# Transposing the late queries of four heads ahead of the expert matmuls, in an attention-and-experts kernel

## Chip, cores, metric

One core of one Trainium2 chip. The metric is the device time of one execution in microseconds (us), the median of several. "PE" is TensorE, "DVE" VectorE, "ACT" ScalarE, "POOL" GpSimd. L252 is line 252 of the kernel; the lines named here are the same ones in both kernels.

## The reference

```python
# q, k, v: (4, 8, 768, 64); centroids: (8, 16, 64)
q_assign = argmax(einsum('bhsd,hcd->bhsc', q_n, c_n))      # rows normalized; likewise k_assign
mask = q_assign[:, :, :, None] == k_assign[:, :, None, :]
attn = softmax(where(mask, scale * q @ k.T, -1e9))          # per batch and head
x = (attn @ v).transpose(0, 2, 1, 3).reshape(3072, 512)
p = domain_probs / (domain_probs.sum(-1, keepdims=True) + 1e-9)
out = sum(p[:, e:e+1] * (relu(x @ w1[e]) @ w2[e]) for e in range(4))
```

Each query and key picks one of 16 clusters; attention runs inside a cluster; four dense experts of 512 to 1024 to 512 follow.

## The kernel before

The order of instructions is fixed by hand. Attention is a generator of "steps" (scores on PE, an exponential on ACT, the product with v on PE two steps later). The first 22 steps run alone; then expert matmuls are woven between further steps. Work on later queries is hung on step numbers (`at_step`) or on a paced generator.

A **turn** takes raw fp32 queries through four 128 x 128 transposes on PE into one PSUM bank and a copy of the bank:

```python
        def turn(self, y, copy, shared=False):          # class Assign, cut
            tp = self.bank()                            # next of self.tags
            for x in range(m):
                for i in range(self.i0, self.i1):
                    nc.tensor.matmul(tp[:, c0:c0 + 128], raw[...][:, y * m + x, i * 128:(i + 1) * 128],
                                     ident, is_transpose=True)              # L242
            t32 = moe.tile([128, DM], F32, name="t32q", tag="oacc", bufs=4)
            copy(t32, tp[:, :m * w])                                        # L252
            ...
        # cast: copies 64 rows of t32 to bf16, on GpSimd                    # L260
```

Each pair of heads is normalized on DVE and turned by PE for the experts:

```python
                        def finish():                                       # cut
                            nc.vector.reciprocal(zr, av[:, :, :, D:D + 1])              # L683
                            nc.vector.tensor_tensor(xn, av[...], zr..., op=ALU.mult)    # L685
                            def turn():                                     # a step or two later
                                nc.tensor.matmul(tp[...], xn[...], identb, is_transpose=True)  # L692
                                dve(xTs[u][...], tp[...])                               # L697
```

The expert weights psb come from four small DVE operations (`probs`: L856, L857, L859, L861). Where things hang:

```python
    at_step = {
        ...
        19: lambda: (qc.onehot(), qc.keep(), qc.send_all()),
        21: probs,
        86: lay_late_constants,
    }
    def late_queries():                  # paced over steps 22 to 32, among the experts
        load_raw()
        for y in (0, 1):
            qd.turn(y, dve, True)
            yield
        casts(qd, (0, 1))
        load_raw(3)
        qd.scores(dve)
        yield
        ...
```

The softmax here doesn't subtract the row's maximum and nothing guards it: scores larger than these inputs give would overflow.

Of the kernel before, what the change touches and what calls it, by code (L numbers as in the profile page):

```python
# [20 lines left out]
def kernel(  # L21
# [22 lines left out]
    QT = A // 2  # L44
# [29 lines left out]
    act, dve, pool = nc.scalar.copy, nc.vector.tensor_copy, nc.gpsimd.tensor_copy  # L74
# [35 lines left out]
    def late(t, b):  # L110
        x = KF[b % 2].rearrange("p h r c -> p (h r c)")
        n = NP * A * 128
        return x[:, t * n:(t + 1) * n].rearrange("p (x i r c) -> p x i r c", i=QT, r=2, c=128)
# [15 lines left out]
    def load_part(b, t, g, js=slice(0, HG), c=slice(0, A * D)):  # L129
        nc.sync.dma_start(  # L130
            out=raw[b, t, g][:, js, c],
            in_=(q, k, v)[t][b, g * HG:(g + 1) * HG]
            .rearrange("h (p a) d -> p h (a d)", p=128)[:, js, c])

    def take_raw():
        nonlocal loaded
        x = ORDER[loaded]
        loaded += 1
        raw[x] = raws.tile([128, HG, A * D], F32, name="raw")
        return x  # L140

    def load_raw(n=1, upto=len(ORDER)):
        for _ in range(n):
            if loaded < upto:
                load_part(*take_raw())
# [198 lines left out]
    class Crossed(Assign):  # L344
# [41 lines left out]
        def casts(self):  # L386
            y = self.g * HG // 2
            if self.b < ROWS:
                for r in range(2):
                    self.cast_half(r)  # L390
                return
            dve(late(self.t, self.b)[:, y:y + HG // 2], self.rows_of())
# [413 lines left out]

    k0, k1 = Assign(0, 1, 0, ("s", "mo", "mo", "mo")), Assign(0, 1, 1, ("s", "misc"))
    qa, qb = Assign(0, 0, 0, ("av",), 0, 1), Assign(0, 0, 1, ("mo",), 0, 1)
    qc, qd = Assign(0, 0, 0, ("misc", "mo"), 1, QT), Assign(0, 0, 1, ("misc",), 1, QT)
    for j in range(HG):  # L810
        k0.turn(j, act)
    lay_centroids()
# [40 lines left out]
    def probs():  # L853
        nonlocal psb
        dps = consts.tile([128, B * A], F32, name="dps")
        nc.vector.tensor_reduce(dps, dp.rearrange("p b a e -> p (b a) e"), axis=AX.X, op=ALU.add)  # L856
        nc.vector.tensor_scalar_add(dps, dps, 1e-9)  # L857
        dpr = consts.tile([128, B * A], F32, name="dpr")
        nc.vector.reciprocal(dpr, dps)  # L859
        psb = consts.tile([128, B * A, E], F32, name="psb")  # L860
        nc.vector.tensor_mul(psb, dp.rearrange("p b a e -> p (b a) e"),  # L861
                             dpr[:, :, None].broadcast_to([128, B * A, E]))

    psb = None
    def late_casts():
# [16 lines left out]
        14: lambda: (casts(qc, (0, 1)), qc.scores(dve)),  # L882
        16: lambda: (qc.back(), qc.top()),
        19: lambda: (qc.onehot(), qc.keep(), qc.send_all()),
        21: probs,
        86: lay_late_constants,
    }

    def late_queries():
        load_raw()  # L890
        for y in (0, 1):
            qd.turn(y, dve, True)
            yield
        casts(qd, (0, 1))
        load_raw(3)
        qd.scores(dve)
        yield
        qd.back()
        qd.top()
        yield  # L900
        qd.onehot()
        qd.keep()
        qd.send_all()
        yield
    S1 = PER_U + PAUSE
    gens.append(Paced(late_queries(), 5, S1 - 6, S1 + 4))
    for b in range(1, B):
        gens.append(Paced(assigns(b), XSTEPS[b], PER_B * (b - 1) if b > 1 else S1 + 7,
# [55 lines left out]
```

## Time and profile before

| | before |
|---|---|
| median of the first three runs | 472.22 us (472.22 to 472.25) |
| span in the profile | 470.4 us |
| PE busy | 463.2 us, 98% |
| chain that ended last, on PE | 95% |

The span is PE's time; every other engine has slack in the mean (ACT is busy 59% of the span, DVE 48%, POOL 41%). So the change is read from PE's idle moments. The prediction shows the lines. Two of its terms come back below: the **stretch** from the attention transposes at 26.7 us (L692) to the first expert matmul of the second unit (L739, at 35 us), in which everything that the change moves lies, and the four small operations in it:

```profile
28.76 0.24 DVE L856 TENSOR_REDUCE dps<-dp 128x24 f32<-128x96 f32 x1
29.03 0.18 DVE L857 TENSOR_SCALAR dps<-dps 128x24 f32<-128x24 f32 x1
29.25 0.30 DVE L859 RECIPROCAL dpr<-dps 128x24 f32<-128x24 f32 x1
29.58 0.26 DVE L861 TENSOR_TENSOR psb<-dp,dpr 128x96 f32<-128x96 f32 x1
```

(start, duration, engine, line). From the first to the L683 behind them, at 29.76, it is 1.00 us.

### The profile page before, as it was taken

Reading aid. Unit: us, or ns where it says so; the run is one execution under the profiler, and the core shown is the slowest. Engines: PE = TensorE matmul, PEld = TensorE weight load, DVE = VectorE, ACT = ScalarE, POOL = GpSimd, SP = SyncE. Lnnn points to the kernel's source line nnn. Section 1 sums busy time; section 2 is a strip of 40 time slices with the busy share of each in tenths; the row PEclk is TensorE's granted clock in tenths of the full one; section 3 lists DMA queues with packets and bytes.
Section 4 is the critical chain, followed back from the end, with each engine's and each line's share of the span. In section 5 each row is a group of like instructions: output and inputs, shape, how many; then the busy total and the mean of one; then the engine's idle time right before and its main releaser. Section 6 shows DMA issues by size and latency. Waiting matters only on the chain.

```text
span 470.4 us, 11349 instructions
## 1 busy us (share of the span) xinstructions
PE 463.2 (98%) x4505; PEld 329.1 (70%) x4505; DVE 227.4 (48%) x554; ACT 276.9 (59%) x502; POOL 194.8 (41%) x301
## 2 busy tenths in 40 slices
PE   8999999999999999999999999999999999999996
PEld 5778777767767766777776667766766666667665
DVE  5964723542325563321234463523778767674112
ACT  5767675445655655566565656656665675664342
POOL 5936779275355593450433942000233232230000
PEclk9999999999999999999999999999999999999999
DMA  8999966996645941503666844220100100100101
GB/s 277 262 211 339 216 99 120 236 127 182 144 68 127 182 114 32 144 18 61 169 123 127 133 106 151 71 75 11 52 13 8 54 11 10 33 29 11 46 2 45
DMA packets 82381, 49.85 MB, mean 106 GB/s; under 512 B 57944, under 2 KB 77080, under 8 KB 82328
## 3 DMA queue, kind: packets, MB, share of 16 engines
q1 hardware_dynamic: 73080, 39.80, 35.1%
q0 software_dynamic: 8576, 9.25, 11.0%
q8 instruction: 35, 0.57, 0.5%
q14 instruction: 18, 0.15, 0.1%
q10 hardware_dynamic: 672, 0.08, 0.1%
HBM read 37.31 MB, written 6.30 MB: 93 GB/s over the span
## 4 chain that ended last, share of the span: by engine, by line
PE 95%; DVE 2%; DMA 1%; issue 0%; ACT 0%; SPq 0%; ACTq 0%
PE ps_mo L739 36%; PE ps_mo L758 35%; PE ps_s L649 9%; PE ps_av L676 7%; PE ps_s L562 1%; DMA kf<-oht 1%; PE ps_misc L562 1%; PE ps_s L87 1%; PE ps_mo L406 1%; PE ps_mo L242 1%; PE ps_misc L406 1%; DVE kf L315 1%; PE ps_misc L242 1%; PE ps_mo L267 0%; PE ps_misc L267 0%; DVE oh L287 0%
## 5 line engine op out<-in xcount | busy, mean ns | idle before, releaser
L655 ACT ACTIVATE at<-ps_s 128x512 bf16<-128x512 f32 x252 | 147.6, 596 | 115.5 <-PE ps_s L649 100.1
L739 PE MATMUL ps_mo<-xT,w1b 128*128 128x256 bf16 (+1 forms) x1664 | 195.9, 264 | 0.0
L758 PE MATMUL ps_mo<-w2b,hT 128*128 128x512 bf16 (+2 forms) x784 | 190.0, 375 | 0.0
L739 PEld LDWEIGHTS <-w1b 128*128 128x128 bf16 x1664 | 146.1, 98 | 24.8 <-issue 1.2
L745 ACT ACTIVATE hT<-ps_mo 128x512 bf16<-128x512 f32 x192 | 114.7, 598 | 60.5 <-PE ps_mo L739 57.7
L767 DVE SCALAR_TENSOR_TENSOR oacc<-ps_mo,psb,oacc 128x512 f32<-128x512 f32 (+1 forms) x74 | 54.3, 734 | 125.3 <-PE ps_mo L758 125.1
L758 PEld LDWEIGHTS <-hT 128*128 128x128 bf16 x784 | 66.9, 98 | 57.8 <-issue 3.1
L649 PE MATMUL ps_s<-qf,kf 80*128 80x256 bf16 (+1 forms) x456 | 82.7, 267 | 0.8 <-ACT at L655 0.4
L676 PEld LDWEIGHTS <-at 128*128 128x128 bf16 x1152 | 69.9, 97 | 15.3 <-issue 1.7
L676 PE MATMUL ps_av<-vx,at 128*128 128x65 bf16 x1152 | 80.3, 193 | 0.0
L662 POOL TENSOR_TENSOR at<-at,same 128x512 bf16<-128x512 bf16 x24 | 28.2, 1177 | 98.5 <-ACT at L655 83.0
L649 PEld LDWEIGHTS <-kf 80*128 80x128 bf16 x456 | 42.1, 98 | 20.6 <-issue 1.4
L380 POOL COPY t<-t 128x768 uint16<-128x768 uint16 x40 | 44.3, 1127 | 0.0
L579 DVE TENSOR_SCALAR same<-qf,late 128x256 bf16<-128x256 bf16 x144 | 39.0, 323 | 0.0
L662 DVE TENSOR_TENSOR at<-at,same 128x512 bf16<-128x512 bf16 x48 | 21.6, 450 | 25.9 <-ACT at L655 25.9
L364 POOL COPY h<-raw 128x768 uint16<-128x768 uint16 x24 | 20.3, 864 | 30.4 <-DMA raw<-in_k_dram 16.7
L361 POOL COPY h<-raw 128x768 uint16<-128x768 uint16 x16 | 13.1, 829 | 39.3 <-DMA raw<-in_q_dram 32.3
L765 DVE TENSOR_SCALAR oacc<-ps_mo,psb 128x512 f32<-128x512 f32 x18 | 13.5, 748 | 27.0 <-PE ps_mo L758 27.0
L683 DVE RECIPROCAL zr<-ps_av 128x4 f32<-128x4 f32 (+1 forms) x50 | 8.9, 178 | 33.3 <-PE ps_av L676 33.2
L336 POOL DMA_DIRECT2D qf<-oht x40 | 20.4, 519 | 7.5 <-DVE oht L313 3.9
L422 POOL COPY st<-sct 128x384 uint16<-128x384 uint16 x16 | 11.0, 736 | 28.8 <-DMA sct<-scs 28.8
L685 DVE TENSOR_TENSOR xn<-ps_av,zr 128x256 bf16<-128x256 f32 (+1 forms) x50 | 20.7, 414 | 1.7
(130 smaller groups left out, 263.2 us busy)
## 6 DMA issues: line engine op xcount, KB each, us to landing
raw<-in_v_dram SPq DMA_DIRECT2D x8, 768.0 KB, 5.4
out_dram<-oacc SPq DMA_DIRECT2D x23, 256.0 KB, 2.0
raw<-in_k_dram SPq DMA_DIRECT2D x7, 768.0 KB, 7.5
raw<-in_q_dram SPq DMA_DIRECT2D x6, 768.0 KB, 5.7
w1b<-in_moe_w_dram POOLq DMA_DIRECT2D x4, 1024.0 KB, 12.3
w2b<-in_moe_w_dram POOLq DMA_DIRECT2D x4, 1024.0 KB, 17.6
qf<-nos SPq DMA_DIRECT2D x2, 768.0 KB, 5.2
xT<-xn SPq DMA_TRANSPOSE x80, 2.4
```

The lines of the kernel that those rows point to most:

```text
L336: (nc.gpsimd if self.b or self.i0 and self.g else nc.sync).dma_start(out=self.rows(slice(D, D + CL), j, r), in_=self.oht[p0:p0 + CL, :self.w])
L380: pool(self.all[:, y * w:(y + 1) * w].bitcast(U16)[:, z::2], self.t16[:, (2 * z + y) * w:(2 * z + y + 1) * w])
L579: nc.vector.tensor_scalar(same[:, x * 256:(x + 1) * 256], clusters(b)[:, g, w, k // 2, k % 2, :], key_nos[b % 2][:, g, 8 * i + 4 * (k // 2 ...
L649: nc.tensor.matmul(sp[:, x * n:(x + 1) * n], KF[b % 2][:K, h, r, i * 128:(i + 1) * 128], QF[b % 2][:K, h, rs[0]:rs[-1] + 1, w * 128:(w + 1 ...
L655: nc.scalar.activation(at, sp, ACT.Exp, scale=scale)
L662: (nc.gpsimd if n4 in POOL_STEPS else nc.vector).tensor_tensor(at, at, same_cluster(b, w, cur), op=ALU.mult)
L676: nc.tensor.matmul(av[:, h % 2, m, :], at[:, c0:c0 + 128], VX[b % 2][:, h, 2 * i + r, :], start=(first and x == 0 and m == 0), stop=(last ...
L685: nc.vector.tensor_tensor(xn[:, :nr].rearrange("p i j d -> p j i d"), av[:, :, :, :D], zr.broadcast_to([128, 2, nr, D]), op=ALU.mult)
L739: nc.tensor.matmul(ph[:, x * n:(x + 1) * n], W1[e][:, i, (f + x) * 128:(f + x + 1) * 128], xT[:, i, :], start=(i == 0), stop=(i == ND - 1))
L745: nc.scalar.activation(ht, ph, ACT.Relu)
L758: nc.tensor.matmul(po, hT[f // per][:, c0:c0 + 128], W2[e][:, f, c], start=(f == 0), stop=(f == NF - 1))
L767: nc.vector.scalar_tensor_tensor(oacc[:, c], po, pap, oacc[:, c], op0=ALU.mult, op1=ALU.add)
```

## The change

Both turns of the late queries of heads 4 to 7 (`qd`) go ahead of the experts, where PE has idle moments; their casts follow at once. The intent is to take 8 transposes out of the stretch in which PE never waits.

```diff
-    qc, qd = Assign(0, 0, 0, ("misc", "mo"), 1, QT), Assign(0, 0, 1, ("misc",), 1, QT)
+    qc, qd = Assign(0, 0, 0, ("misc", "mo"), 1, QT), Assign(0, 0, 1, ("misc", "mo"), 1, QT)
...
-        21: probs,
+        18: lambda: qd.turn(0, dve, True),
+        21: lambda: (qd.turn(1, dve, True), casts(qd, (0, 1)), probs()),
...
     def late_queries():
         load_raw()
-        for y in (0, 1):
-            qd.turn(y, dve, True)
-            yield
-        casts(qd, (0, 1))
+        yield
         load_raw(3)
+        yield
         qd.scores(dve)
```

## The prediction

> **What bounds the kernel now.** I read the page's busy times and chain first, then the waits of TensorE (PE) in two stretches, then the timeline of the place that the diff touches.
>
> ```profile
> PE 463.2 (98%) x4505; PEld 329.1 (70%) x4505; DVE 227.4 (48%) x554; ACT 276.9 (59%) x502; POOL 194.8 (41%) x301
> ...
> PE 95%; DVE 2%; DMA 1%; issue 0%; ACT 0%; SPq 0%; ACTq 0%
> ```
>
> PE is the bound, by busy share and by the chain that ended last. So the question is which idle moments of PE the change fills or makes. The waits of PE from 17 to 60 us are these; from 60 us to the end the same view has no line at all.
>
> ```profile
> PE ps_misc L296 <- DVE oh L287: 0.6, 2, 0.4
> PE ps_s L649 <- ACT at L655: 0.4, 2, 0.3
> PE ps_mo L692 <- DVE xn L685: 0.3, 1, 0.3
> PE ps_s L649 <- DMA kf<-oht: 0.3, 1, 0.3
> ```
>
> After about 38 us PE never waits. A delay there goes to the end undiminished, and so does a gain. PE's idle time ahead of the experts (which start at 28.77) is small: about 0.3 us in each of few places. The place itself, from the timeline (start, duration, engine, line):
>
> ```profile
> 26.72 0.23 PE L692 MATMUL ps_mo<-identb,xn 128*128 128x128 bf16 x1 [0.28 <-DVE xn L685]
> 26.79 0.39 PE L649 MATMUL ps_s<-qf,kf 80*128 80x128 bf16 x4
> 27.45 0.29 DVE L313 TENSOR_SCALAR oht<-ps_mo 128x256 bf16<-128x256 bf16 x1 [0.24 <-PE ps_mo L296]
> 27.80 0.17 DVE L683 RECIPROCAL zr<-ps_av 128x2 f32<-128x2 f32 x1
> 27.92 0.39 PE L649 MATMUL ps_s<-qf,kf 80*128 80x128 bf16 x4 [0.16 <-ACT at L655]
> 28.00 0.29 DVE L685 TENSOR_TENSOR xn<-ps_av,zr 128x128 bf16<-128x128 f32 x1
> 28.35 0.23 PE L692 MATMUL ps_mo<-identb,xn 128*128 128x128 bf16 x1
> 28.77 0.61 PE L739 MATMUL ps_mo<-xT,w1b 128*128 128x128 bf16 x8
> 29.56 0.63 PE L242 MATMUL ps_misc<-ident,raw 128*128 128x128 f32 x4
> 29.76 0.17 DVE L683 RECIPROCAL zr<-ps_av 128x2 f32<-128x2 f32 x1
> 29.97 0.29 DVE L685 TENSOR_TENSOR xn<-ps_av,zr 128x128 bf16<-128x128 f32 x1
> 30.03 0.61 PE L739 MATMUL ps_mo<-xT,w1b 128*128 128x128 bf16 x8
> 30.23 0.69 DVE L252 COPY t32q<-ps_misc 128x512 f32<-128x512 f32 x1
> 30.83 0.22 PE L692 MATMUL ps_mo<-identb,xn 128*128 128x128 bf16 x1
> 31.45 0.63 PE L242 MATMUL ps_misc<-ident,raw 128*128 128x128 f32 x4
> 31.92 0.61 PE L739 MATMUL ps_mo<-xT,w1b 128*128 128x128 bf16 x8
> ```
>
> A "turn" is four fp32 transposes on PE (L242) and a copy of the bank on VectorE (L252). The reader is to see its two turns at 29.56 and 31.45, between expert matmuls, and the other VectorE work: each attention output goes L683, L685 on VectorE, L692 on PE, so L692 can make PE wait for VectorE (it did at 26.72).
>
> [...] four transposes show 0.63 us, but the next matmul starts 0.47 us after the first (29.56 to 30.03), so a turn costs PE 0.47 us, and 8 bf16 matmuls of 128 columns 0.45 us. [...] the scores behind the waiting L692 started only after it. So a copy put ahead of L683 on VectorE delays L692, and transposes put behind a waiting L692 don't fill its wait. [...]
>
> **The change, part by part.** Nothing is added or removed: the order of instructions shows equal counts on every engine, and differences on PE and VectorE only (GpSimd, ScalarE and the DMA queues keep theirs). What moves: turn 0 goes behind the L692 of 26.72, ahead of the scores of 26.79; turn 1 behind the L692 of 28.35, ahead of the scores of 28.41. On VectorE, copy 0 comes ahead of the L313 of 27.45; copy 1 comes ahead of the four small operations (28.76 to 29.76, the expert weights psb) and thus ahead of the L683 of 29.76. The banks of this head group alternate between "mo" and "misc"; I read from the built program what each first write of a bank waits for, and each is a reader done long before.
>
> PE moves 2 x 0.47 = 0.94 us of work from the saturated stretch to the stretch before. The gain is what of it falls into idle time; I replay the stretch with the trace's durations. Turn 0 runs 26.80 to 27.27. It stands behind the wait at 26.72, so does not fill it. The scores move from 26.79 to 27.27, their exponential from 27.27 to 27.75, and the scores that wait for that exponential from 27.92 to 28.40: this gap of 0.33 (27.59 to 27.92 before, counted by streaming time) moves along and isn't filled. Both shift by 0.47 to 0.48. VectorE: copy 0 starts at 26.80 + 0.63 + 0.04 = 27.47; start to start such copies took 0.59 to 0.70 in this trace, so L313 is at 28.06 to 28.17, L683 at about 28.4, L685 at 28.6 to 28.9, and L692 at about 28.95 (0.06 after L685's end). PE would be ready at 28.74 (28.40 + 0.22 + 0.12). That is a wait of 0.2 against 0.09 before: **+0.1**.
>
> Turn 1 runs from 29.02 to 29.49, the experts start at about 29.84, 1.07 later than before. Copy 1 starts at 29.02 + 0.67 = 29.69; the four small operations at 30.3 to 30.4; they take 1.00; L683 at 31.3 to 31.4; L685 ends 0.50 later, at 31.8 to 31.9; L692 at about 31.9. In PE's order that L692 comes 30.83 + 1.07 - 0.47 (the turn no longer at 29.56) = 31.43. So PE, until then without a gap, waits some **+0.45**. Then turn 1's old place (31.45) falls away, -0.47. The next L692 (33.35) finds its L685 done: no VectorE copy stands at 32.19 any more. The score matmuls (L267), now in bank "mo", wait for an ACT result of 33.8 and come at 34.1. Nothing else changes; the gap before the one-hot transposes at 37.20 stays.
>
> Sum: +0.94 (turns early) - 0.94 (turns gone later) + 0.1 + 0.45 + 0 filled = +0.55 us. [...] I add a little for start-to-start times on the longer side: +0.6, so 472.22 + 0.6 = **472.8 us**.
>
> **Rivals.** First, the intent: the turns fall into idle time of PE ahead of the experts. For it: there are gaps of 0.28 and 0.33 close by, and ScalarE, which the scores feed, has slack. At most 0.94 is gained, 471.3 us. Against: the turns stand behind one wait, and push the matmuls that start the other. Second, VectorE becomes the bound for longer: copy 0 also delays the one-hot result (L313), whose eight transfers feed the scores at 35.40, and the late raw loads behind these on the same queue. For: the transfers start 0.6 late, and if these scores waited for them, another 0.5 to 1 us would be lost, 473.5 us. Against: the page has 4.8 us to landing, the first two are due at about 34, and those scores need only them. Third, a wash: VectorE overlaps better than I replay (the small operations or L683 start sooner), the new wait vanishes: 472.2 to 472.3 us. I hold the replay at about 65%, the wash 15%, the gain 10%, the larger loss 10%.
>
> **Range and chances.** No rival reaches 2% (9.4 us): the work moved is 0.94 us, and the largest loss named is 1.3. So "within 2%" is 0.99. The range goes from the wash, 472.1, to a replay with each wait 0.3 longer, 473.4.
>
> **What would show it.** In the profile after: PE's wait at L692 for VectorE's L685 appears once more, some 0.4 us at about 31.9 (step two); the wait at 26.72 is still there, with L242 right behind it; the gap before the scores at 28.4 is still there (nothing filled); experts start at 29.8 instead of 28.77; PE's position at the second half of the first expert is some 0.55 later than before and stays so to the end. Wrong it would be if the L692 of 31.9 shows no wait, if the gaps at 26.7 to 28.4 vanish from PE's waits, or if PE gets new waits after 38 us, which the replay says it does not.

## The result, and the profile after

After: 473.48 us median of 4 runs (472.98 to 473.64); before, beside it: 472.24 (472.22 to 472.28). The ratio is 1.0024, with a 95% interval of 1.0007 to 1.0042. Ratios here are the mean time of one kernel's runs over that of the other's of the same rounds, so not quite the ratio of the medians. It is within 2%, and slower.

PE's waits from 17 to 60 us in the changed kernel (engine, line, whom it waited for: us in total, times, longest):

```profile
PE ps_mo L692 <- DVE xn L685: 0.8, 1, 0.8
PE ps_s L649 <- DMA kf<-oht: 0.6, 2, 0.4
PE ps_s L649 <- ACT at L655: 0.4, 2, 0.3
PE ps_misc L296 <- DVE oh L287: 0.4, 1, 0.4
PE ps_mo L296 <- DVE oh L287: 0.2, 1, 0.2
```

Before, the one wait at an L692 was the 0.3 us of 26.72. Now it is 0.8 us, at a later L692: the one of 32.61 in the timeline of the changed kernel (lines picked from the view):

```profile
27.16 0.23 PE L692 MATMUL ps_mo<-identb,xn 128*128 128x128 bf16 x1
27.23 0.61 PE L242 MATMUL ps_mo<-ident,raw 128*128 128x128 f32 x4
28.81 0.38 PE L649 MATMUL ps_s<-qf,kf 80*128 80x128 bf16 x4 [0.16 <-ACT at L655]
29.24 0.23 PE L692 MATMUL ps_mo<-identb,xn 128*128 128x128 bf16 x1
29.30 0.61 PE L242 MATMUL ps_misc<-ident,raw 128*128 128x128 f32 x4
30.02 0.69 DVE L252 COPY t32q<-ps_misc 128x512 f32<-128x512 f32 x1 [0.29 <-PE ps_misc L242]
30.10 0.61 PE L739 MATMUL ps_mo<-xT,w1b 128*128 128x128 bf16 x8
30.63 0.24 DVE L856 TENSOR_REDUCE dps<-dp 128x24 f32<-128x96 f32 x1
30.77 1.26 POOL L260 CAST qf<-t32q 64x512 bf16<-64x512 f32 x2 [0.88 <-DVE t32q L252]
30.90 0.51 DVE L857 TENSOR_SCALAR dps<-dps 128x24 f32<-128x24 f32 x1
31.45 0.30 DVE L859 RECIPROCAL dpr<-dps 128x24 f32<-128x24 f32 x1
31.79 0.36 DVE L861 TENSOR_TENSOR psb<-dp,dpr 128x96 f32<-128x96 f32 x1
32.07 0.16 DVE L683 RECIPROCAL zr<-ps_av 128x2 f32<-128x2 f32 x1
32.26 0.29 DVE L685 TENSOR_TENSOR xn<-ps_av,zr 128x128 bf16<-128x128 f32 x1
32.61 0.23 PE L692 MATMUL ps_mo<-identb,xn 128*128 128x128 bf16 x1 [0.76 <-DVE xn L685]
```

The reader is to see three things. The two turns stand right behind an L692, and the gap before the scores of 28.81 is still there. The small operations now come behind the copy of 30.02, and two of them are longer: L857 took 0.51 us (before 0.18) and L861 0.36 (before 0.26), while two casts ran on GpSimd (0.61 us each, the first to about 31.4, where L857 ended too). From L856 to L683 it is 1.44 us instead of 1.00. And L692 waits for the L685 at the end of this row. (The first L692, of 27.16, did not wait in this profile, since a transfer had just held PE for 0.21 us; in the repeat below it waits 0.34 us again.)

Where the time went, by the stretch: its end is this line, before and after,

```profile
34.95 0.61 PE L739 MATMUL ps_mo<-xT,w1b 128*128 128x128 bf16 x8
36.27 0.61 PE L739 MATMUL ps_mo<-xT,w1b 128*128 128x128 bf16 x8
```

so 26.72 to 34.95 is 8.23 us before, 27.16 to 36.27 is 9.11 after, **+0.88 us**. The other part of the 1.24 us between the medians lies ahead of it: the stretch starts 0.44 us later, and of this 0.4 was lost in the first 8 us, ahead of anything that the change touches. The first nine transposes of the kernel (of keys), before and in the changed kernel:

```profile
4.63 1.74 PE L242 MATMUL ps_mo<-ident,raw 128*128 128x128 f32 x9
4.58 2.12 PE L242 MATMUL ps_mo<-ident,raw 128*128 128x128 f32 x9
```

The experiments had to tell whether this belongs to the change.

### The profile page after: what moved, and what is told of

Same layout as the page of the kernel before. It is cut to its first block, busy times and chain, and to the rows that moved or that the text cites. A ratio compares the mean times of both kernels' runs of the same rounds, so it can differ in the third digit from the quotient of the medians. Undisturbed runs are those within 1.5% of the kernel's fastest.

```text
span 471.7 us, 11348 instructions
## 1 busy us (share of the span) xinstructions
PE 463.2 (98%) x4505; PEld 329.7 (70%) x4505; DVE 227.1 (48%) x554; ACT 277.0 (59%) x502; POOL 194.3 (41%) x301
## 4 chain that ended last, share of the span: by engine, by line
PE 95%; DVE 3%; DMA 1%; issue 0%; ACT 0%; SPq 0%; DVEq 0%; ACTq 0%
PE ps_mo L739 35%; PE ps_mo L758 35%; PE ps_s L649 9%; PE ps_av L676 7%; PE ps_s L562 1%; DMA kf<-oht 1%; PE ps_mo L242 1%; PE ps_misc L562 1%; PE ps_s L87 1%; PE ps_mo L406 1%; PE ps_mo L267 1%; PE ps_misc L406 1%; DVE kf L315 1%; DVE oh L287 0%; DVE mx L284 0%; PE ps_misc L242 0%
## 5 line engine op out<-in xcount | busy, mean ns | idle before, releaser
L683 DVE RECIPROCAL zr<-ps_av 128x4 f32<-128x4 f32 (+1 forms) x50 | 8.9, 178 | 34.9 <-PE ps_av L676 34.9
L685 DVE TENSOR_TENSOR xn<-ps_av,zr 128x256 bf16<-128x256 f32 (+1 forms) x50 | 20.7, 414 | 1.7
```

Source lines behind the costliest of these rows:

```text
L685: nc.vector.tensor_tensor(xn[:, :nr].rearrange("p i j d -> p j i d"), av[:, :, :, :D], zr.broadcast_to([128, 2, nr, D]), op=ALU.mult)
```

## The experiments

All gave correct results. Each was timed in five rounds against the kernel before on its chip. The times turned out to have an uneven start (below), so the stretch in the trace, which does not hold it, is the better measure of a few tenths. For the last versions, whose first turn lies ahead of the stretch, a longer one is used, from the score transposes at about 25 us (L276) to the same end. Each stretch is read from one profiled execution. Two pairs show how well it repeats: 8.23 in before and in hold24, which has the same stretch, and 9.11 and 9.10 in the changed kernel and its repeat. The longer one also holds waits for a transfer, which differ: probs_late, with the short stretch of before, has 10.25 there against 10.02.

A diff below that shows `- 21: probs` or `hold_clock` is against the kernel before, any other against the changed kernel.

| kernel | times, us (lowest, median, highest) | stretch, us | longer stretch, us |
|---|---|---|---|
| before (29 runs beside these, on three chips; a median for each) | 472.03; 472.49, 472.18, 472.19; 473.03, and one of 474.42 | 8.23 | 10.02 |
| after_again | 472.98, 473.06, 473.65 | 9.10 | 10.90 |
| probs_late | 472.06, 472.17, 472.96 | 8.22 | |
| casts_act | 472.60, 472.84, 473.30 | 8.67 | |
| before_probs_late | 472.30, 472.72, 473.24 | 8.44 | |
| turn0_early | 472.18, 472.46, 472.71 | 8.20 | |
| turn1_early | 472.91, 473.06, 473.56 | 9.07 | |
| turns_ahead | 471.92, 471.99, 472.10 | | 9.60 |
| turns_ahead_again | 471.73, 471.92, 472.27 | | 9.58 |
| ahead_probs_kept | 471.82, 471.94, 472.35 | | 9.90 |
| turns_ahead_split | 471.50, 471.82, 471.86 | | 9.18 |
| hold24 | 472.85, 473.26, 473.60 | 8.23 | 10.03 |

The run of 474.42 shows a mean granted clock of 0.995, the other runs of before 0.999 or 1.000; it is in the ratios of turns_ahead, ahead_probs_kept, turn0_early and turn1_early. Without it, the plain ratios of the means would be 0.9994, 0.9995, 1.0004 and 1.0018.

**after_again: the changed kernel once more.**

> The changed kernel once more, for its spread. In its profile the first nine transposes ran 0.4 us slower than in the kernel before, ahead of anything that the change touches. Theory A (the change itself costs 0.9 us, at the attention transposes of 32.6 us; the slow start is separate and differs from run to run): times between 473.0 and 473.7, and a profile whose delay against before grows by 0.9 us between 26 and 34 us, whatever its start. Rival B (the slow start is most of the loss): runs with a fast start come within 0.3 us of before, at about 472.5.

Ratio 1.0016 (1.0002 to 1.0030). Four of five runs came at 472.98 to 473.09; of the nine runs of before beside them, four came at 472.10 to 472.19 and the rest up to 473.03. So the low groups are 0.9 us apart, and both kernels have slower runs: the slow start is no part of the change. Its profiled run, 473.03, had a fast start:

```profile
4.58 1.63 PE L242 MATMUL ps_mo<-ident,raw 128*128 128x128 f32 x9
```

and a stretch of 9.10 us. Theory A holds (0.87 us in the stretch, whatever the start); rival B falls.

**probs_late: the small operations behind the third normalization.**

```diff
-        21: lambda: (qd.turn(1, dve, True), casts(qd, (0, 1)), probs()),
+        21: lambda: (qd.turn(1, dve, True), casts(qd, (0, 1))),
+        23: probs,
```

> The changed kernel, with the four small VectorE operations (expert weights psb) moved behind the normalization of the third output, so that copy 1 no longer pushes them ahead of it. Theory A: the wait of TensorE of 0.76 us at the attention transposes near 32.6 us vanishes, the kernel is 0.9 us faster than the changed one run beside it, and within 0.2 us of before (apart from the start). Rival C (the early transposes themselves cost TensorE time that is not won back): the time stays at that of the changed kernel, 0.9 us or more above before.

Ratio 0.9997 (0.9985 to 1.0010). The stretch is 8.22 us, that of before. The profiled run (472.96) is the slowest of the five, with a slow start (2.14 us for the nine transposes) and a longer wait for a transfer ahead of the stretch; the other four came at 472.06 to 472.19. The attention transposes no longer wait:

```profile
31.99 0.22 PE L692 MATMUL ps_mo<-identb,xn 128*128 128x128 bf16 x1
```

So the whole loss is that one wait. And with it gone the change is a wash: 0.9 us of transposes moved ahead of the experts win nothing, since they fill no idle moment there.

**casts_act: the casts on ScalarE, later.**

```diff
-        21: lambda: (qd.turn(1, dve, True), casts(qd, (0, 1)), probs()),
+        21: lambda: (qd.turn(1, dve, True), probs()),
...
+        for y in (0, 1):
+            for r in range(2):
+                qd.cast(y, r, act)
         qd.scores(dve)
```

> The changed kernel, with the four casts of the late queries on ScalarE, later, instead of on GpSimd at 28.6 to 32.0 us. In the changed kernel two of the small operations took 0.51 and 0.36 us (0.18 and 0.26 before) while a GpSimd cast ran. Theory A1 (the casts block them): they are back at 0.18 and 0.26 us, the wait near 32.6 us shrinks from 0.76 to about 0.35 us, and the time falls by 0.4 us against the changed kernel. Rival (their length is of another cause, such as their distance to the copy): they stay at 0.5 and 0.36 us and the time stays.

The stretch is 8.67 us: 0.44 less than in the changed kernel, 0.44 more than before. In its timeline both operations are short again, and the wait is 0.32:

```profile
30.77 0.18 DVE L857 TENSOR_SCALAR dps<-dps 128x24 f32<-128x24 f32 x1
...
31.32 0.26 DVE L861 TENSOR_TENSOR psb<-dp,dpr 128x96 f32<-128x96 f32 x1
...
32.04 0.23 PE L692 MATMUL ps_mo<-identb,xn 128*128 128x128 bf16 x1 [0.32 <-DVE xn L685]
```

Ratio 1.0009 (0.9997 to 1.0022): by the times alone, this isn't told from before, nor clearly from the changed kernel; by the trace it is half-way. So half of the loss (0.44 us) is the order on DVE, and half goes with GpSimd's casts at the same time. How a cast lengthens an operation on DVE, no trace shows; the traces show which operations took longer. In the changed kernel L857, a tensor_scalar on 24 numbers per partition, took 0.51 us and ended 0.03 us behind the first cast. L856, a reduction, kept its 0.24 us in the run probs_late, where it ran at 31.81 us under the second of two casts that began at 31.07. L859, a reciprocal, kept its 0.30 us beside a cast in the changed kernel (31.45) and in ahead_probs_kept (30.24).

casts_act takes the casts to another engine and to a later time at once, so by itself it shows only that they did it. The other traces close the gap. In six profiles whose timelines show L857 beside a cast (after, after_again, probs_late, before_probs_late, turn1_early, ahead_probs_kept), it took anything from 0.29 to 0.51 us, and ended 0.03 to 0.04 us behind the end of that cast each time; in four whose timelines show none beside it (before, casts_act, turns_ahead, turn0_early) it took 0.18. L861 beside a cast took 0.35 or 0.36 us and ended 0.11 to 0.12 behind it (five profiles), and 0.26 in the five others of these ten. A length of another cause, the rival, would not follow the cast's end.

**before_probs_late: the control.**

```diff
-        21: probs,
+        23: probs,
```

> Control: the kernel before, with the small VectorE operations moved to the same later place. There the attention transposes at 30.8 us did not wait. Theory A: no change, within 0.1 us of before. If it gains as much as the same move gains in the changed kernel, then the move is good by itself and says nothing of the change.

The expectation of "no change" missed: the stretch is 8.44, 0.21 more than before. In the trace the moved operations now fall under the casts of turn 0 (L857 0.51, L861 0.36 us), and the copy of turn 1 and the fourth normalization come later behind them. But the control says what it was made for: the move is no gain by itself. The ratio, 1.0005 (0.9993 to 1.0018), tells nothing.

**turn0_early and turn1_early: one turn each.** In turn0_early one turn is hung on step 18, in turn1_early one on step 21; the second one stays in the generator, with its casts for both. (turn0_early has the two alternating banks of the changed kernel, turn1_early the one bank of before.)

```diff
+        18: lambda: qd.turn(0, dve, True),                  # turn0_early
-        21: probs,                                          # turn1_early
+        21: lambda: (qd.turn(0, dve, True), probs()),       # turn1_early
...
-        for y in (0, 1):                                    # both
-            qd.turn(y, dve, True)
-            yield
+        yield
+        qd.turn(1, dve, True)
+        yield
```

> Turn 0 alone at its new place (ahead of the experts), turn 1 where the kernel before has it. Theory A: turn 0 fills no gap and copy 0 is off the path of the later normalization, so its 0.45 us are only moved: within 0.1 us of before, no new wait near 31 us. Rival (either early turn costs half of the loss): 0.45 us slower.

> One turn alone at the place of turn 1 (the second of the two is left where the kernel before has it). Theory A: this copy stands ahead of the small operations and its casts block two of them, so the whole loss is here: a wait of about 0.8 us at the attention transposes near 31 us, 0.85 us slower than before. Rival: 0.45 us slower.

The stretch is 8.20 us with turn 0 early (before 8.23) and 9.07 with the one at the place of turn 1 (after 9.11); ratios 1.0001 (0.9987 to 1.0015) and 1.0015 (1.0000 to 1.0031). The whole loss is the place of turn 1, ahead of the small operations; its L857 took 0.51 us there too. Turn 0 is only moved.

**turns_ahead: a step earlier.** If an early turn gains only what falls into a gap, it must come ahead of the wait, not behind it.

```diff
-        18: lambda: qd.turn(0, dve, True),
+        17: lambda: qd.turn(0, dve, True),
-        21: lambda: (qd.turn(1, dve, True), casts(qd, (0, 1)), probs()),
+        20: lambda: (qd.turn(1, dve, True), casts(qd, (0, 1))),
+        23: probs,
```

> A version that should beat both: turn 0 one step earlier, ahead of the scores that precede the attention transposes of 26.7 us, so that TensorE does it while VectorE normalizes; turn 1 one step earlier, ahead of the scores that wait for an exponential (the gap of 0.33 us at 27.6); the small operations behind the third normalization. Theory A (early turns gain only what falls into a gap of TensorE): turn 0 is free, turn 1 costs about 0.12 of its 0.45 us, so 0.6 us faster than before between runs of equal start, some 471.5 us, and 1.5 us faster than the changed kernel. Rival (the scores delayed by turn 0 delay their exponential and all after it): within 0.2 us of before.

The longer stretch is 9.60 us, 0.42 less than before; the expected 0.6 was too much. The waits at the attention transposes are gone, and one of the two for an exponential. The missing 0.2 is in the first expert group, 0.83 us instead of 0.61:

```profile
29.24 0.83 PE L739 MATMUL ps_mo<-xT,w1b 128*128 128x128 bf16 x8
```

Its fourth matmul reads the second output, whose copy (L697, 29.36 to 29.57) now stood on DVE behind the copy of turn 1 (from 28.76). By time, the ratio is 0.9991 (0.9977 to 1.0005): not told from before. In order, though, its six runs (471.92 to 472.10) lie below ten of before's eleven (472.11 and more; one is 472.03).

**ahead_probs_kept: the same, with `21: probs` left.**

> The same, but with the small VectorE operations left where the change leaves them, ahead of the third normalization. Theory A: copy 1 now comes earlier, so these end at about 30.4 us even when a GpSimd cast blocks two of them, and the attention transposes near 30.5 us wait some 0.4 us: 471.9 us. If the place of the turns is all that matters, the time is that of the run before this one.

The longer stretch is 9.90: 0.30 more than without, where 0.4 was expected. L857 took 0.38 us, L861 0.36, and L692 came 0.30 us behind what precedes it on PE (31.40, where the products before it were through at 31.10). The times of the two (471.94 and 471.99 in the median) don't tell them apart; the start is uneven by more.

**turns_ahead_split and turns_ahead_again.** In the first, PE's part of turn 1 stays on step 20, and its copy and casts go to step 21 (the diff is against turns_ahead):

```diff
-        20: lambda: (qd.turn(1, dve, True), casts(qd, (0, 1))),
+        20: lambda: qd.turn(1, lambda *x: held.append(x), True),
+        21: lambda: (dve(*held.pop()), casts(qd, (0, 1))),
```

> The version with both turns one step earlier, with one more repair: in its trace the first expert group took 0.83 us instead of 0.61, since copy 1 stood on VectorE ahead of the copy of the second output that this group reads. Here TensorE's part of turn 1 stays and its copy goes behind that one. Theory A: the group is back at 0.61 us, and from the score transposes at 25 us to the second unit's first expert matmul it takes 9.4 us (before 10.02, both turns ahead 9.60): 0.6 us faster than before at equal starts. Rival (copy 1, later, delays the third normalization again): a wait at the attention transposes near 31 us, and no gain over 9.60.

> The version with both turns one step earlier once more: its trace says 0.42 us faster than before, its times only 0.2, with a start of middling speed in its profile (nine first transposes 2.01 us; 1.63 in fast starts, 2.14 in slow ones). If the start is what hides the rest, runs with a fast start come at 471.7 us, and the profile shows 9.6 us for the stretch again.

The split version beats both kernels: 471.82 us median, ratio 0.9985 (0.9972 to 0.9999), longer stretch 9.18 us, its first expert group at 0.61 us again. It is 0.2 shorter than expected: the four scores behind turn 0 took 0.39 us here, and 0.65 in turns_ahead, where the last of them started late (0.56 in its repeat). The program has these scores wait for one-hot keys sent by DMA, and in four other profiles such a wait is named there (`DMA kf<-oht`, 0.21 to 0.74 us), so a sooner landing is likely, though not shown, and need not repeat. It also gives some back at 40.85 us, in a wait that no other kernel here had, for the next batch's keys:

```profile
40.85 0.55 PE L242 MATMUL ps_misc<-ident,raw 128*128 128x128 f32 x3 [0.26 <-DMA raw<-in_k_dram]
```

The repeat of turns_ahead had its stretch at 9.58 again, and two runs at 471.73 and 471.74, 0.4 below the low group of before (472.13 to 472.19). Its profiled run, 472.27, had the slowest start of all (2.15 us). The ratio is 0.9989 (0.9977 to 1.0002). So the uneven start can hide a gain of this size in the medians.

**hold24: the uneven start.** The kernel begins with 16 matmuls on zeros; here 24, in the kernel before.

```diff
-    hold_clock(16)
+    hold_clock(24)
```

> The kernel before with 24 instead of 16 matmuls on zeros ahead of the first transposes, to see what the uneven start is. If it is the rate at which TensorE runs in its first microseconds (the first transposes came at 0.21 us each in slow starts and sped up at another moment in each run), the first nine transposes, which start some 1.7 us later, take at most 1.6 us in any run, and the times of the runs lie within 0.3 us of each other, about 1.5 us above before. If the uneven start comes from the loads, the spread stays.

The ratio is 1.0016 (1.0003 to 1.0029). The nine transposes took 1.27 us in the profile, but the times spread over 0.75 us (472.85 to 473.60), as much as before's, where 0.3 was expected, and the median lies 1.07 us above before's, where 1.5 was. By the expectation's own words a spread that stays speaks for the loads. Yet it does not settle it: in the profile all 24 matmuls came about 0.21 us apart, 5.3 us in all, as the 16 do, and PE sped up only with the transposes behind them; if it does so at another moment in each run, the 24 end at another moment too. What stands is a correlation. Of the ten other experiments, the three profiled runs whose nine transposes took 1.60 to 1.70 us lie within 0.06 us of their kernels' fastest run; those with 1.81 to 2.15 lie 0.1 to 0.9 above. The traces show the delay itself: over all twelve profiles with 16 matmuls, the score transposes near 25 us (L276) start at 24.79 to 24.98 us where the nine took 1.60 to 1.81, and at 25.14 to 25.45 where they took 2.01 to 2.15. What sets PE's rate at the start, no run shows: the transposes came about 0.21 us apart at first in a slow start (after: 5.65 to 6.50 us, four of them) and 0.11 to 0.12 later, among other matmuls, while the granted clock read 1.00 from the start in the six profiles that were read by stages (before, after and the first four experiments), whose nine transposes took 1.63 to 2.14 us.

## Why the prediction was right, and where it was off

The mechanism was right, and so was the direction. One term of its sum was too small by half. That a copy ahead of L683 on DVE delays L692 was the expectation; in the changed kernel the copy, the four small operations, L683 and L685 started one after the other from 30.02, and L692 came at 32.61.

- **"Turns fill no gap"**: right. After, both turns stand behind an L692, the gap before the scores of 28.81 is there, and probs_late (8.22 against 8.23 us) shows that moving the turns alone is a wash.
- **"A turn costs PE 0.47 us"**: 0.44 and 0.45 at the new places (27.23 to 27.67, 29.30 to 29.75), so 0.05 less for both together.
- **"+0.1" at the second L692**: nothing. The scores, from 28.81, and the products behind them take PE to 29.15, and L692 comes at 29.24: 0.09, as before. The next operation on DVE started 0.60 us after the copy did, and L683 0.20 behind that; the prediction left 0.59 to 0.70 open for the first and took some 0.3 for the second.
- **"+0.45" at the third L692**: this is the mis-sized term. Without a wait it would follow the products of 31.57 at 31.69; it came at 32.61, so it lost **0.92 us** (the profile counts 0.76, from the end of its record of these products, at 31.85). The prediction's step "the four small operations take 1.00" failed: they took 1.44. It moved the casts on GpSimd with the turns, and said that GpSimd's order doesn't change, but not that its casts would run at the same time as these operations, nor that two of them would take longer there (0.51 us instead of 0.18, 0.36 instead of 0.26). casts_act takes just that away and gets 0.44 back; what it leaves at the third L692, 0.44 in the stretch and 0.05 for the shorter turns, is about the 0.45 of the replay.
- **The sum**: 0.92 for the wait, less 0.05 for the shorter turns, is 0.87; the stretch has 0.88. Predicted was +0.6.
- **The range**: 472.1 to 473.4 left out the spread that goes with the uneven start, up to about 0.9 us between runs of one kernel. The first runs of before were all alike within 0.06 us and gave no hint of it. So the median of 473.48 consists of the 0.88 us and about 0.4 us of start. That it is just the figure of the rival of the transfers (473.5) is a coincidence: its mechanism did not come (below).
- **Rivals**: the gain (turns in idle time) did not come at these places, but did when the turns were put ahead of the waits. The transfers (one-hot rows later) did not matter: the scores that need them, at 36.72 us, did not wait. No new wait of PE appeared after 38 us; the one at L296, 38.52, is that of 37.20 before.

## What to carry to other kernels

Here work moved to a busy engine's idle time helped only where it stood *ahead* of the wait in that engine's order (turns_ahead: 0.42 us less in the longer stretch); behind it, it just moved the wait along (probs_late: 8.22 us in the stretch, 8.23 before). Look also at the engine that takes the result: here a copy ahead of a normalization on VectorE, with the casts that followed it, cost PE 0.92 us, as much as the eight transposes take. And when a producer moves, its followers on other engines move with it: check what they will run beside, GpSimd with VectorE above all (here L857 took 0.51 us instead of 0.18 beside a cast).
